# Reordering the two ends of a spectral and windowed-attention kernel: first loads from two queues, zero matmuls ahead of the first product, one pad a step earlier, and output projections in front of a block's last sums

## The chip, the cores and the metric

The kernel runs on one core of a Trainium2 chip. The metric is device time in microseconds for one execution. Five engines matter: TensorE (PE; its weight loads are PEld), VectorE (DVE), ScalarE (ACT), GpSimd (POOL) and SyncE (SP), which issues nearly all of this kernel's DMAs.

## The reference

```python
# x: 2048 x 512; 32 heads of 16; window of 256 keys, causal
g = sigmoid((x * gate_w).sum(-1, keepdims=True))
a = einsum("bsd,ed->bse", x, dft_hid_re);  b = einsum("bsd,ed->bse", x, dft_hid_im)
y = einsum("ts,bse->bte", dft_seq_re, a) - einsum("ts,bse->bte", dft_seq_im, b)
q, k, v = split(x @ wqkv)
scores = where(0 <= i - j < 256, q @ k.T * 16**-0.5, -1e9)
att = (softmax(scores) @ v).reshape(S, D) @ wo
out = g * y + (1 - g) * att
```

So the output is a gated mix of a two-sided Fourier product (real part) and a sliding-window attention with an output projection. Everything is float32. Each large product is made of three matmuls in a faster 32-bit format: both operands are split into a high part (a cast) and a low part (the rest), and the terms high x high, high x low and low x high are summed (`TERMS`).

## The kernel before, in words

**Attention.** Queries are cut into 4 head groups times 32 blocks of 64 positions, 128 blocks in all; the main loop runs over them with index `n`. Per step, four pairs `p` make scores S (`s_pair`, line 319: a query block, padded so that two heads share it, against a ring of keys), and VectorE adds the mask and takes the row maximum, ScalarE the exponential's sum. Eighteen steps behind (`LAG`, `k = n - LAG`) come the transposed scores T (`t_pair`, line 384: a key block in `PAD[1, k]` against the ring of queries), their exponential, and the product with V (`pv`, line 411). `make_pad(i, n)` writes a padded block: for T one half is VectorE's (line 304) and the other is ScalarE's (line 302). In the kernel before, T's first pad is made at the start of step `n = 18` (`k == 0`), each later one a step ahead of its use.

**Dense work.** All else is a generator, `dense()`, that yields between groups of matmuls; `fill(n)` draws a fixed number of them per half pair into the attention loop. It runs the first Q/K product (`qk_first`, line 226), V's blocks (`v_proj`, line 260), the other Q/K products (line 238), the hidden-side Fourier products (line 260 too), and the sequence-side Fourier sums (`c_block`, line 442): 16 output blocks `tb` for the first half, then 16 for the second, each 48 matmuls of 512 columns. What is left of it when the attention loop ends runs by itself.

**The start.** Before that loop, the first pieces of the Q/K weights (`wqk`, four of 128x256) and of x transposed (`xT`, four of 128x512) are loaded in turn from SP's queue, split on ScalarE (line 136 and `split`, line 80) and VectorE (lines 83 and 138), and multiplied.

**The end.** When the attention is done, `attention_done` splits the output projection's weights into `fin`. From then on `add_r` (line 566) combines a block's Fourier sum with the first half's and calls `wo_block`: load the attention output of the block, split it into a buffer named `raw`, 12 matmuls (line 604), mix with line 606, store. One block that had been waiting is projected in front of each.

**What sets the order.** TensorE's order is the order of the trace (`manual_schedule`). On the other engines a planner orders the instructions by its own simulated time, except inside the block at lines 127 to 138. `mark` remembers the last instruction of an engine, and `with behind(...)` or `late(...)` puts what follows behind it in that engine's order. The pool `ev` has 5 buffers, `raw` 2, the split weights `hi` and `lo` 3 each; the PSUM pool `ps_a` has 4 banks shared by S, T and the projections.

Of the kernel before, what the change touches and what calls it, by code (L numbers as in the profile page):

```python
# [14 lines left out]
P = 128  # L15
# [3 lines left out]
NG = 4  # L19
# [4 lines left out]
BIG = 1e30  # L24
SCALE = 0.25
LAG = 18
BEHIND = 4
FILL_FIRST, FILL_PROJ, FILL_SEQ = 3.0, 3.5, 3.6

# [2 lines left out]
def fnet_window_mix(ctx: ExitStack, tc: tile.TileContext, xT, x, wqk, wv, wr, wi, cr, ci, wo, gw, out):  # L32
# [21 lines left out]
    def ld(dst, src):  # L54
        return nc.sync.dma_start(dst, src)

    def store(dst, src):
        mark("sp", ld(dst, src))

    def f(ap):  # L60
        return ap.bitcast(F32)
# [56 lines left out]
    def split_x(ss, dks, act=False):  # L118
        for dk in dks:
            XT[dk, ss] = big.tile([P, 2, 512], F32R, name="big")  # L120
            split(XT[dk, ss][:, 0], XT[dk, ss][:, 1], XRAW.pop((dk, ss)), act)
# [5 lines left out]
    with tc.manual_schedule(engines={mybir.EngineType.Activation, mybir.EngineType.DVE, mybir.EngineType.SP}):  # L127
        wraw, *xraw = [pt_raw() for _ in range(3)]
        wq0 = [st.tile([P, 1024], F32R, name=h) for h in ("hi", "lo")]
        for dk in range(DK):  # L130
            ld(wraw[:, dk * 256:dk * 256 + 256], wqk[0][:, dk * 256:dk * 256 + 256])
            XRAW[dk, 0] = xraw[dk // 2][:, HALVES[dk % 2]]
            ld(XRAW[dk, 0], xT[0, dk])
        for dk in range(DK):
            c = slice(dk * 256, dk * 256 + 256)
            nc.scalar.copy(wq0[0][:, c], wraw[:, c])
            split_x(0, (dk,), True)
            nc.vector.tensor_sub(wq0[1][:, c], wraw[:, c], f(wq0[0][:, c]))


    NPAD = 3
# [51 lines left out]

    def gate_load(j):
        if j == 0:
            ld(gwb, bass.AP(tensor=gw.tensor, offset=gw.offset, ap=[[0, P], [1, D]]))
        GX[j] = st.tile([P, 1024], F32, name="raw", bufs=2)
        for c in range(2):
            ld(GX[j][:, HALVES[c]], x[2 * j + c])
# [275 lines left out]
    def late(fn, *args):  # L475
        with behind("act", "dve"):
            return fn(*args)

    def dense():
        wraw = [load_raw(wv[i]) for i in range(2)]  # L480
        qk_first(wq0)
        wvs = [split_raw(r, True) for r in wraw]
        load_x(1, 0)
        load_x(1, 1)
        yield
        for ss in range(4):
            if ss:
                yield from qk_proj(0, ss, wq0)
            for c in range(4):
                yield from v_proj(ss * 4 + c, wvs)  # L490
                have.add(("v", ss * 4 + c))
                if c == 1:
                    have.add(("qk", 0, ss))
                if ss < 3:
                    if c in (1, 2):
                        late(split_x, ss + 1, (2 * c - 2, 2 * c - 1), ss == 0)
                        if ss < 2:
                            load_x(ss + 2, c - 1)
                elif c == 0:
                    raw = load_raw(wqk[1])  # L500
                    wraw = [load_raw(wi[0])]
                elif c == 2:
                    w = late(split_raw, raw)
        for g in range(1, NG):
            for ss in range(4):
                yield from qk_proj(g, ss, w)
                have.add(("qk", g, ss))
                if g == 1:
                    if ss == 0:
                        wraw.append(load_raw(wi[1]))  # L510
                    elif ss < 3:
                        if ss == 1:
                            ws = []
                        ws.append(late(split_raw, wraw[ss - 1]))
                        if ss == 1:
                            raw = load_raw(wqk[2])
                        else:
                            gate_load(0)
                elif g == 2:
                    if ss == 0:  # L520
                        raw = load_raw(wqk[3])
                        wraw = [load_raw(wr[0])]
                    elif ss == 2:
                        nextw = late(split_raw, raw)
                        wraw.append(load_raw(wr[1]))
                elif ss in (0, 2):
                    if ss == 0:
                        ws = []
                    ws.append(late(split_raw, wraw[ss // 2]))
            if g == 1:  # L530
                for sb in range(16):
                    yield from ab_proj(1, sb, ws)
                    if sb == 1:
                        nextw = late(split_raw, raw)
                    if sb % 2 == 0 and sb < 14:
                        gate_load(sb // 2 + 1)
                    if sb % 2:
                        late(gate, sb - 1)
                        late(gate, sb)
            if g < 3:  # L540
                w = nextw
        ab = {}
        for sb in range(16):
            if sb >= 4:
                ab[sb] = big.tile([P, 2, 512], F32R, name="big")
            yield from ab_proj(0, sb, ws, ab.get(sb))
        for sc in range(4):
            ab[sc] = load_ab(0, sc)
        have.add("proj")
        def store_r(tb, ps):  # L550
            t = ev.tile([P, 512], F32, name="ev")
            nc.scalar.activation(t, ps, AF.Copy, scale=g1[:, tb:tb + 1])
            ld(r_scr[0][tb], t)

        get = c_pieces([*((0, k) for k in (*range(28), 28, 30, 29, 31)),
                        *((1, k) for k in (0, 2, 1, 3, *range(4, 32)))])
        for tb in range(14):
            yield from c_block(get, 0, tb, ab, store_r)
        yield from c_pair(get, 0, 14, ab, store_r, True)
        ab = nxt  # L560
        wait = []

        def add_r(tb, ps):
            r = ev.tile([P, 512], F32, name="ev")
            ld(r, r_scr[0][tb])
            nc.vector.scalar_tensor_tensor(r, ps, g1[:, tb:tb + 1], r, op0=OP.mult, op1=OP.add)
            if FIN:
                if wait:
                    wo_block(wait.pop(0))
                wo_block(tb, r)  # L570
            else:
                ld(r_scr[1][tb], r)
                wait.append(tb)

        yield from c_pair(get, 1, 0, ab, add_r)
        for tb in range(2, 16):
            yield from c_block(get, 1, tb, ab, add_r)
        while wait:
            wo_block(wait.pop(0))

    FIN = []

    def attention_done():
        fin = const.tile([P, 2, 2, 2, 512], F32R, name="fin", tag="ring0")
        for j in range(2):
            raw = st.tile([P, 1024], F32, name="raw", bufs=2)
            ld(raw, wo[j])
            for c in range(2):
                split(fin[:, j, c, 0], fin[:, j, c, 1], raw[:, c * 512:c * 512 + 512])
        FIN.append(fin)  # L590

    def wo_block(tb, r=None):
        if r is None:
            r = ev.tile([P, 512], F32, name="ev")
            ld(r, r_scr[1][tb])
        oraw = ev.tile([P, NG, P], F32, name="ev")
        ld(oraw, o_scr[tb // 4][:, :, tb % 4 * P:tb % 4 * P + P].rearrange("g p t -> p g t"))
        o = st.tile([P, 2, NG, P], F32R, name="raw", bufs=2)
        split(o[:, 0], o[:, 1], oraw[:], True)
        ps = ps_a.tile([P, 512], F32, name="t", tag="st")  # L600
        n = 0
        for g in range(NG):
            for a, b in TERMS:
                nc.tensor.matmul(ps, o[:, a, g], FIN[0][:, g // 2, g % 2, b], start=n == 0, stop=n == 11)  # L604
                n += 1
        nc.vector.scalar_tensor_tensor(r, ps, g0[:, tb:tb + 1], r, op0=OP.mult, op1=OP.add)
        ld(out[tb], r)


    stream = dense()  # L610
# [34 lines left out]
    for n in range(N + LAG + 2):  # L645
# [13 lines left out]
            v_spread(k + 2)  # L659
        if n == 0:  # L660
            make_pad(0, 0)
        if k == 0:
            make_pad(1, 0)
        for p in range(NP):
            if n < N:
                s_pair(n, p)
            fill(n)
            if 0 <= k < N:
                t_pair(k, p)
            if p == 0:  # L670
                make_pad(0, n + 1)
                if k >= 0:
                    make_pad(1, k + 1)
            fill(n)
            if p == 2 and n % 2:
                for j in (k - 2, k - 1):
                    if 0 <= j < N:
                        pv(j)
                if n % 8 == 1 and 1 < n <= N + 1:
                    m_rows(n // 8 - 1)  # L680
                    l_rows(n // 8 - 1)
# [47 lines left out]
```

## Time and profile before

| | |
|---|---|
| median of 3 runs | 880.83 us (879.98 to 882.15) |
| the profiled execution | 881.33 us, span 879.5 us |
| mean granted TensorE clock | 0.996 |
| TensorE busy | 866.5 us, 5184 matmuls |
| VectorE, ScalarE, GpSimd busy | 600.1, 585.3, 385.0 us |
| DMA | 152.13 MB, mean 173 GB/s |

The page gives the busy time of each engine, the span in 40 slices (each digit the busy share of a slice in tenths), and the chain of work that ended last. The list of waits says which engine sat idle, at which line, and who released it: total us, number of times, longest. The timeline has one row per instruction or group: start, duration, engine, line, operation, output and inputs, and in brackets the idle time before it and what ended it. A row of a table by windows has the stretch, its length, the busy time and count of PE, PEld, DVE, ACT and POOL, the granted clock, the DMA engines' share and GB/s. "L260" is line 260 of the kernel.

### The profile page before, as it was taken

To read this page: it belongs to the slowest core of one execution; us is meant where nothing else is said; L and a number is where in the kernel's file an instruction comes from. 1 tells how busy PE (TensorE), PEld (TensorE's weight loads), DVE (VectorE), ACT (ScalarE), POOL (GpSimd) and SP (SyncE) were. 2 spreads that over 40 slices of the span, in tenths; PEclk is the share of its full clock that TensorE was granted. 3 is DMA by queue.
4 is the path that set the end of the run, shared out by engine and by line. 5 is a ranking of instruction groups with operands and counts; after the bars stand their busy time and mean duration, and the time that the engine had idled before them with its cause. 6 is when DMAs were issued, how large, how long until landed. Compare 5 with 4: busy or idle time off the path is not lost.

```text
span 879.5 us, 17216 instructions
## 1 busy us (share of the span) xinstructions
PE 866.5 (99%) x5184; PEld 692.2 (79%) x5184; DVE 600.1 (68%) x1965; ACT 585.3 (67%) x1794; POOL 385.0 (44%) x1069
## 2 busy tenths in 40 slices
PE   7999899999999999999999999999999999999997
PEld 6888678777877878787778787877878777788885
DVE  4688788777887677777777777778776443454342
ACT  5488788889888887888878878888776444100010
POOL 9100165555544447564455566545656664000000
PEclk9999899999999999999999999999999999999999
DMA  7877668775766136543544353579643323455452
GB/s 265 261 228 214 198 205 272 233 237 174 221 207 210 45 99 200 147 138 120 175 131 140 127 148 115 143 230 348 211 143 126 130 92 126 137 174 156 149 159 88
DMA packets 89823, 152.13 MB, mean 173 GB/s; under 512 B 26753, under 2 KB 35457, under 8 KB 89729
## 3 DMA queue, kind: packets, MB, share of 16 engines
q1 hardware_dynamic: 89728, 151.02, 55.0%
q8 instruction: 41, 0.67, 0.3%
q14 instruction: 54, 0.43, 0.2%
HBM read 103.81 MB, written 47.19 MB: 172 GB/s over the span
## 4 chain that ended last, share of the span: by engine, by line
PE 98%; DMA 1%; ACT 1%; issue 0%; DVE 0%; SPq 0%; ACTq 0%
PE dc L442 41%; PE dab L260 10%; PE dqk L238 10%; PE s L319 9%; PE o L411 8%; PE t L384 8%; PE dv L260 5%; PE t L604 5%; PE s L226 1%; DMA ev<-o_scr 1%; PE s L343 0%; PE s L331 0%; DMA pt<-xT 0%; ACT sm L324 0%; ACT raw L80 0%
## 5 line engine op out<-in xcount | busy, mean ns | idle before, releaser
L442 PE MATMUL dc<-big,hi 128*128 128x512 f32 x1024 | 354.9, 395 | 0.0
L390 POOL TENSOR_SCALAR_AFFINE_SELECT pt<-pt 64x128 f32<-64x128 f32 x512 | 192.7, 376 | 292.1 <-ACT pt L385 276.2
L324 ACT ACTIVATE sm<-sm,nm 128x320 f32<-128x320 f32 (+4 forms) x512 | 276.8, 542 | 59.4 <-DVE nm L321 56.7
L321 DVE CUSTOM_DVE_ANT_0 sm<-s,mask 128x320 f32<-128x320 f32 (+4 forms) x512 | 232.3, 462 | 118.3 <-PE s L319 94.0
L385 ACT ACTIVATE pt<-t 128x320 f32<-128x320 f32 (+4 forms) x512 | 208.0, 412 | 81.3 <-PE t L384 78.7
L442 PEld LDWEIGHTS dc<-big,hi 128*128 128x128 f32 x1024 | 186.8, 188 | 28.0 <-issue 1.5
L442 PE MATMUL dc<-big,lo 128*128 128x512 f32 x512 | 202.6, 396 | 0.0
L319 PE MATMUL s<-ring,pad 128*128 128x320 f32 (+4 forms) x512 | 160.7, 314 | 0.0
L394 POOL TENSOR_SCALAR_AFFINE_SELECT pt<-pt 64x128 f32<-64x128 f32 x448 | 160.3, 358 | 0.0
L384 PE MATMUL t<-ring,pad 128*128 128x320 f32 (+4 forms) x512 | 154.8, 302 | 3.0 <-ACT pad L302 2.6
L304 DVE TENSOR_SCALAR pad<-ring,half 96x256 fp32r<-96x256 f32 x384 | 121.8, 359 | 19.7 <-PE t L384 19.2
L319 PEld LDWEIGHTS s<-ring,pad 128*128 128x128 f32 x512 | 96.4, 188 | 38.7 <-issue 9.3
L384 PEld LDWEIGHTS t<-ring,pad 128*128 128x128 f32 x512 | 96.5, 189 | 20.3 <-ACT pad L302 2.9
L442 PEld LDWEIGHTS dc<-big,lo 128*128 128x128 f32 x512 | 96.2, 188 | 16.5 <-issue 1.6
L83 DVE TENSOR_TENSOR lo<-raw,hi 128x512 fp32r<-128x512 f32 x146 | 100.0, 711 | 0.3 <-ACT hi L80 0.3
L324 ACT ACTIVATION_READ_ACCUMULATOR sm<-sm,nm 128x1 f32 x512 | 98.1, 192 | 0.0
L82 DVE CAST hi<-raw 128x512 fp32r<-128x512 f32 x142 | 56.8, 437 | 51.8 <-PE dc L442 31.8
L260 PE MATMUL dab<-hi,big 128*128 128x512 f32 x256 | 91.1, 396 | 0.0
L238 PE MATMUL dqk<-big,hi 128*128 128x512 f32 x240 | 87.3, 399 | 0.0
L80 ACT CAST raw<-ev 128x512 fp32r<-128x512 f32 x16 | 9.9, 622 | 110.0 <-DVE lo L83 72.3
L411 PE MATMUL o<-pt,vpad 128*32 128x320 f32 (+4 forms) x1408 | 78.6, 352 | 0.0
L411 PEld LDWEIGHTS o<-pt,vpad 128*32 128x32 f32 x1408 | 36.0, 109 | 36.9 <-issue 19.8
(79 smaller groups left out, 823.1 us busy)
## 6 DMA issues: line engine op xcount, KB each, us to landing
qk_scr<-hl SPq DMA_DIRECT2D x32, 512.0 KB
ring<-qk_scr SPq DMA_DIRECT2D x32, 512.0 KB
raw<-cr SPq DMA_DIRECT2D x32, 512.0 KB
raw<-ci SPq DMA_DIRECT2D x32, 512.0 KB
ab_scr<-hl SPq DMA_DIRECT2D x20, 512.0 KB
big<-ab_scr SPq DMA_DIRECT2D x20, 512.0 KB
ring<-qk_scr SPq DMA_DIRECT2D x32, 256.0 KB
r_scr<-ev SPq DMA_DIRECT2D x25, 256.0 KB
```

What stands on the lines that cost most here:

```text
L238: nc.tensor.matmul(ps, w[a][:, c:c + 128], XT[dk, ss][:, b], start=n == 0, stop=n == 11)
L260: nc.tensor.matmul(ps, XT[dk, ss][:, a, c * 128:(c + 1) * 128], wh[b], start=n == 0, stop=n == 11)
L304: nc.vector.tensor_scalar(dst, src, half[:96, h:h + 1], None, op0=OP.mult)
L319: nc.tensor.matmul(ps[:, :w], PAD[0, n][:, p], ring[1][:, p, k0:k0 + w], start=True, stop=True)
L321: mark("dve", nc.vector.tensor_tensor_reduce(out=sm[:, :w], in0=ps[:, :w], in1=mask[:, WIN - w:], scale=1.0, scalar=3e38, op0=OP.add, op1= ...
L324: mark("act", nc.scalar.activation(sm[:, :w], sm[:, :w], AF.Exp, bias=nm[:, c], scale=-1.0, accum_out=l[:, c]))
L384: nc.tensor.matmul(ps[:, :w], PAD[1, n][:, p], ring[0][:, p, q0:q0 + w], start=True, stop=True)
L385: nc.scalar.activation(pt[:, p, :w], ps[:, :w], AF.Exp, scale=-1.0)
L390: nc.gpsimd.affine_select(a, a, pattern=[[0, 2], [1, 64]], compare_op=OP.is_ge, fill=0.0, base=0, channel_multiplier=-1)
L394: nc.gpsimd.affine_select(a, a, pattern=[[0, 2], [-1, 64]], compare_op=OP.is_gt, fill=0.0, base=0, channel_multiplier=1)
L411: nc.tensor.matmul(OT[g, sb][32 * p:32 * p + 32, q - sb * 512:e - sb * 512], v2[:, p], pt[:, p, q - q0:e - q0], start=first, stop=kb == 8 ...
L442: nc.tensor.matmul(ps, w[a][:, s8 * 128:(s8 + 1) * 128], ab[SC[i]][:, b], start=i == 0 and a + b == 0, stop=i == 15 and a == 1)
```

## The change

- The first loads: the x blocks 0 and 2 are issued from ScalarE's queue, x 1 and 3 and the weights from SP's. The first x block's high part is cast on VectorE, not on ScalarE.
- A tile of zeros is set by VectorE, and `warm()` issues six matmuls of it ahead of the first product.
- V's weights are loaded behind the last of these loads on SP; their splits are placed behind the first product's evictions (`late`). The gate's weights are loaded behind what SP had been given by then.
- `make_pad(1, 0)` moves from the start of step 18 to the first pair of step 17.
- At the end, `wo_prep` loads and splits the attention output of coming blocks a block ahead, into a tile of 8 slots in the place of the key ring (`ring1`), not in `raw`. `wo_block` runs in front of a block's sums: for the block itself (`half` 0, with the first half's part), and for blocks that were waiting (`half` 1). `add_r` then only adds the sums and stores; for block 15 in two halves, from two queues. Block 10 joins the waiting ones; 11 to 15 have 3, 4, 3, 3 and 3 projections in front.

```diff
+WARM = 6
...
         wq0 = [st.tile([P, 1024], F32R, name=h) for h in ("hi", "lo")]
+        zero = at.tile([P, 512], F32R, name="rl", bufs=1)
+        nc.vector.memset(f(zero[:]), 0.0)
+        for dk in (0, 2, 1, 3):
+            XRAW[dk, 0] = xraw[dk // 2][:, HALVES[dk % 2]]
+            if dk % 2 == 0:
+                nc.scalar.dma_start(XRAW[dk, 0], xT[0, dk])
         for dk in range(DK):
-            ld(wraw[:, dk * 256:dk * 256 + 256], wqk[0][:, dk * 256:dk * 256 + 256])
-            XRAW[dk, 0] = xraw[dk // 2][:, HALVES[dk % 2]]
-            ld(XRAW[dk, 0], xT[0, dk])
+            store(wraw[:, dk * 256:dk * 256 + 256], wqk[0][:, dk * 256:dk * 256 + 256])
+            if dk % 2 == 0:
+                ld(XRAW[dk + 1, 0], xT[0, dk + 1])
         for dk in range(DK):
             c = slice(dk * 256, dk * 256 + 256)
-            nc.scalar.copy(wq0[0][:, c], wraw[:, c])
-            split_x(0, (dk,), True)
-            nc.vector.tensor_sub(wq0[1][:, c], wraw[:, c], f(wq0[0][:, c]))
+            mark("act", nc.scalar.copy(wq0[0][:, c], wraw[:, c]))
+            split_x(0, (dk,), dk > 0)
+            mark("dve", nc.vector.tensor_sub(wq0[1][:, c], wraw[:, c], f(wq0[0][:, c])))
...
         if j == 0:
-            ld(gwb, bass.AP(tensor=gw.tensor, offset=gw.offset, ap=[[0, P], [1, D]]))
+            with behind("sp"):
+                ld(gwb, bass.AP(tensor=gw.tensor, offset=gw.offset, ap=[[0, P], [1, D]]))
...
+    def warm():
+        ps = ps_d.tile([P, 512], F32, name="dv", tag="d")
+        for i in range(WARM):
+            nc.tensor.matmul(ps, zero[:, :128], zero, start=i == 0, stop=i == WARM - 1)
+
     def dense():
-        wraw = [load_raw(wv[i]) for i in range(2)]
+        warm()
+        with behind("sp"):
+            wraw = [load_raw(wv[i]) for i in range(2)]
         qk_first(wq0)
-        wvs = [split_raw(r, True) for r in wraw]
+        wvs = [late(split_raw, r, True) for r in wraw]
...
+        mixed = {}
+
         def add_r(tb, ps):
-            r = ev.tile([P, 512], F32, name="ev")
-            ld(r, r_scr[0][tb])
-            nc.vector.scalar_tensor_tensor(r, ps, g1[:, tb:tb + 1], r, op0=OP.mult, op1=OP.add)
-            if FIN:
-                if wait:
-                    wo_block(wait.pop(0))
-                wo_block(tb, r)
-            else:
+            r = mixed.pop(tb, None)
+            late_r = r is not None
+            if not late_r:
+                r = ev.tile([P, 512], F32, name="ev")
+                ld(r, r_scr[0][tb])
+            for i in range(2 if tb == 15 else 1):
+                c = slice(i * 256, i * 256 + 256) if tb == 15 else slice(0, 512)
+                nc.vector.scalar_tensor_tensor(r[:, c], ps[:, c], g1[:, tb:tb + 1], r[:, c], op0=OP.mult, op1=OP.add)
+                if late_r:
+                    (nc.scalar.dma_start if i else ld)(out[tb][:, c], r[:, c])
+            if not late_r:
                 ld(r_scr[1][tb], r)
                 wait.append(tb)
...
         for tb in range(2, 16):
+            if tb in O:
+                mixed[tb] = wo_block(tb, 0)
+            for w in [w for w in wait if w in O]:
+                wait.remove(w)
+                ld(out[w], wo_block(w, 1))
+            if FIN and tb < 15:
+                for w in (tb + 1, *wait[:-(-len(wait) // (15 - tb))]):
+                    wo_prep(w)
             yield from c_block(get, 1, tb, ab, add_r)
-        while wait:
-            wo_block(wait.pop(0))
...
+        fin = const.tile([P, 4096 + 16], F32R, name="fin", tag="ring0")[:, 16:]
+        fin = fin.rearrange("p (j c h e) -> p j c h e", j=2, c=2, h=2)
+        OS.append(const.tile([P, 8, 2, NG, P], F32R, name="os", tag="ring1"))
...
+    def wo_prep(tb):
         oraw = ev.tile([P, NG, P], F32, name="ev")
         ld(oraw, o_scr[tb // 4][:, :, tb % 4 * P:tb % 4 * P + P].rearrange("g p t -> p g t"))
-        o = st.tile([P, 2, NG, P], F32R, name="raw", bufs=2)
-        split(o[:, 0], o[:, 1], oraw[:], True)
+        O[tb] = OS[0][:, next(slot) % 8]
+        split(O[tb][:, 0], O[tb][:, 1], oraw[:], True)
+
+    def wo_block(tb, half):
+        o = O.pop(tb)
+        r = ev.tile([P, 512], F32, name="ev")
+        ld(r, r_scr[half][tb])
         ps = ps_a.tile([P, 512], F32, name="t", tag="st")
...
-        ld(out[tb], r)
+        return r
...
-        if k == 0:
-            make_pad(1, 0)
...
             if p == 0:
                 make_pad(0, n + 1)
-                if k >= 0:
+                if k >= -1:
                     make_pad(1, k + 1)
```

More of the change, by code (lines that the diff above doesn't have):

```diff
@@ L576, in dense @@
         for tb in range(2, 16):
+            if tb in O:
[6 more added lines that the diff above has]
+                    wo_prep(w)
             yield from c_block(get, 1, tb, ab, add_r)
-        while wait:
-            wo_block(wait.pop(0))
     FIN = []
     def attention_done():
-        fin = const.tile([P, 2, 2, 2, 512], F32R, name="fin", tag="ring0")
+        fin = const.tile([P, 4096 + 16], F32R, name="fin", tag="ring0")[:, 16:]
+        fin = fin.rearrange("p (j c h e) -> p j c h e", j=2, c=2, h=2)
+        OS.append(const.tile([P, 8, 2, NG, P], F32R, name="os", tag="ring1"))
         for j in range(2):
@@ L590, in attention_done @@
         FIN.append(fin)
[L592 to L595, printed above, removed]
+    OS = []
+    O = {}
+    slot = iter(range(99))
+    def wo_prep(tb):
         oraw = ev.tile([P, NG, P], F32, name="ev")
         ld(oraw, o_scr[tb // 4][:, :, tb % 4 * P:tb % 4 * P + P].rearrange("g p t -> p g t"))
-        o = st.tile([P, 2, NG, P], F32R, name="raw", bufs=2)
-        split(o[:, 0], o[:, 1], oraw[:], True)
+        O[tb] = OS[0][:, next(slot) % 8]
[4 more added lines that the diff above has]
+        ld(r, r_scr[half][tb])
         ps = ps_a.tile([P, 512], F32, name="t", tag="st")
```

## The prediction

> **What bounds the kernel now.** I read the page first (busy shares, slices, the chain), then the list of TensorE's waits, then the timeline around each wait.
>
> ```profile
> span 879.5 us, 17216 instructions
> PE 866.5 (99%) x5184; PEld 692.2 (79%) x5184; DVE 600.1 (68%) x1965; ACT 585.3 (67%) x1794; POOL 385.0 (44%) x1069
> PEclk9999899999999999999999999999999999999999
> PE 98%; DMA 1%; ACT 1%; issue 0%; DVE 0%; SPq 0%; ACTq 0%
> ```
> ```profile
> PE s L226 <- ACT big L80: 4.7, 1, 4.7
> PE t L384 <- ACT pad L302: 2.6, 1, 2.6
> PE t L604 <- ACT raw L80: 1.4, 1, 1.4
> ```
>
> TensorE is the chain, and its matmuls are the same before and after but for six of zeros. So there is nothing to win but its idle time and its slow stretches. The second list has all of it: the start (4.7), the first transposed score (2.6), the last projection (1.4), and behind the last matmul a tail. The change touches each.
>
> **The first T (make_pad(1, 0) a step earlier).**
>
> ```profile
> 95.64 0.39 PE L238 MATMUL dqk<-big,hi 128*128 128x512 f32 x1
> 95.87 0.31 PE L319 MATMUL s<-ring,pad 128*128 128x320 f32 x1
> 96.02 0.40 PE L238 MATMUL dqk<-big,hi 128*128 128x512 f32 x1
> 99.02 0.60 PE L384 MATMUL t<-ring,pad 128*128 128x320 f32 x1 [2.60 <-ACT pad L302]
> 99.42 0.63 PE L238 MATMUL dqk<-big,lo 128*128 128x512 f32 x1
> 99.85 0.63 PE L238 MATMUL dqk<-big,hi 128*128 128x512 f32 x1
> ```
> ```profile
> 97.91 0.74 DVE L82 CAST hi<-raw 128x512 fp32r<-128x512 f32 x2
> 98.58 0.34 DVE L304 TENSOR_SCALAR pad<-ring,half 96x256 fp32r<-96x256 f32 x1
> ```
> ```profile
> 99.02:105.02 6.00, 6.00 (x16) 5.04 (x17) 2.17 (x7) 2.39 (x7) 1.09 (x4) 0.50 0.91 235
> ```
>
> The wait is put down to ScalarE's half of the pad, but VectorE's half ends at 98.92, and TensorE starts at 99.02: that is the later one. It stands behind weight splits (97.91). Then comes a second price: from 99.02 to 105.02 the granted clock is 0.50. Those 16 matmuls (ten of 512 columns, six of 320) would take 10 x 0.23 (95.64 to 95.87) + 6 x 0.15 (95.87 to 96.02) = 3.2 us at full clock; they took 6.0, so 2.8 more. The wait costs 2.6 + 2.8 = 5.4 us. In the changed kernel the same two pad pieces are traced behind pair 0 of step 17, so behind what VectorE and ScalarE had been given by then. On VectorE this can be the eviction in the first row below; it ends at 93.47, and T is due at 96.25, so 2.8 us are left for a piece of 0.34.
>
> ```profile
> 92.79 0.68 DVE L90 SCALAR_TENSOR_TENSOR hl<-dqk,hl 128x512 fp32r<-128x512 f32 x1
> ```
>
> Bounds: all of it (-5.4), or nothing if the planner again puts it behind splits (0). I take -5.4, since what it must follow has been done 2.8 us early. Late next are VectorE's reads of the score banks: VectorE is still busy as the gap ends today (97.91 to 98.92), and the four PSUM banks that S and T share cover about two pairs. I take no stall.
>
> The Trainium skill (TensorE: Matmul & The Clock Gate, Why this matters for your kernels) says the clock falls after gaps above about 3 us. Here 2.6 us were followed by 0.50, so the measurement decides; by the rule alone this term would be -2.6 and the sum 877.1.
>
> **The start (two queues, zeros, later V splits).**
>
> ```profile
> 4.10 0.43 SPq L55 DMA_DIRECT2D pt<-xT  x1
> ```
> ```profile
> 1.50:7.50 6.00, 2.78 (x6) 2.00 (x7) 1.26 (x3) 2.90 (x6) 5.68 (x13) 1.00 0.83 250
> ```
> ```profile
> 8.77 0.62 ACT L80 CAST big<-pt 128x512 fp32r<-128x512 f32 x1 [0.22 <-DMA pt<-xT]
> 10.05 2.42 ACT L80 CAST hi<-raw 128x512 fp32r<-128x512 f32 x4 [0.67 <-DMA raw<-wv]
> 12.38 1.09 ACT L86 ACTIVATE hl<-s 128x512 fp32r<-128x512 f32 x2
> 15.60 0.59 ACT L270 COPY ev<-dv 128x512 f32<-128x512 f32 x1 [2.12 <-PE dv L260]
> ```
> ```profile
> 9.42 0.69 DVE L83 TENSOR_TENSOR big<-pt,big 128x512 fp32r<-128x512 f32 x1
> 10.03 0.42 DVE L138 TENSOR_TENSOR lo<-pt,hi 128x256 fp32r<-128x256 f32 x1
> 10.70 2.58 DVE L83 TENSOR_TENSOR lo<-raw,hi 128x512 fp32r<-128x512 f32 x4 [0.26 <-ACT hi L80]
> ...
> 13.80 0.68 DVE L88 TENSOR_TENSOR hl<-s,hl 128x512 fp32r<-128x512 f32 x1
> ```
> ```profile
> 4.72 8.12 PE s L226 x24
> ```
> ```profile
> 12.68 0.39 PE L260 MATMUL dv<-hi,big 128*128 128x512 f32 x1
> ```
>
> Two queues save issue time: the last x block is SP's fifth issue instead of its eighth, so it goes out three issues of 0.43 earlier, near 2.8 instead of 4.10. But the DMA engines are 0.83 busy at 250 GB/s; the eight loads are 4 x (128 + 256) KB = 1.57 MB, 6.3 us from 1.50, so the last cannot land before 7.8; it landed by 8.77. I take 8.3. Behind it stand the cast 0.62, VectorE's 0.69 and 0.42, and four matmuls of 0.23: the first Q/K product ends at 8.3 + 2.6 = 10.9 (bounds 10.4 and 11.4) instead of 12.68, if the array runs at full speed by then. Today the product's 24 matmuls take 8.12 us, 0.34 each against 0.23: part waits, part slow matmuls. For that are the zeros: six at the slow spacing of 0.43 (99.42 to 99.85), 2.6 us from about 1.3, done before 4.72, where the product starts; as long as its first operands are later than 3.9, they cost nothing. If the array stays slow as today, the end stays at 12.68.
>
> What speaks against the gain is `late` on V's weight splits. Today VectorE makes all four low halves (10.70, 2.58) before the Q/K evictions. Now they stand behind both: the second ended at 14.48, 1.80 after the product. The last low half is then ready at 1.80 + 2.58 = 4.38 after the product, and with two matmuls and 0.20 of drain the first V block's copy starts 5.0 after it; today it starts 15.60 - 12.68 = 2.9 after it. So 10.9 + 5.0 = 15.9 against 15.60: +0.3. The bounds are 15.4 (-0.2) and 12.68 + 5.0 = 17.7 (+2.1). I take +0.3, as the middle landing gives it. ScalarE's two issues (0.43 each) stand ahead of its first cast; between 0 and 0.9, I take 0, because the first block's cast moves to VectorE, which idles then, and the first operands are still loading. The gate weights and V's loads, now behind the last wqk load on SP, cost nothing: V's casts come behind the evictions anyway, and the gate is not read until the second group's rows.
>
> The Trainium skill (DMA: Bandwidth & Descriptors, Rules for kernel authors) holds that spreading loads over issuing engines saves only issue time. With the landing left at 8.77 the term would be +0.8 and the sum 874.8.
>
> **The end (projections ahead).**
>
> ```profile
> 851.46 0.62 PE L442 MATMUL dc<-big,hi 128*128 128x512 f32 x2
> ...
> 862.36 8.56 PE L604 MATMUL t<-fin,raw 128*128 128x512 f32 x36
> ...
> 872.29 3.33 PE L604 MATMUL t<-fin,raw 128*128 128x512 f32 x12 [1.37 <-ACT raw L80]
> ```
> ```profile
> 848.85 0.33 SPq L55 DMA_DIRECT2D raw<-ci  x1
> ```
> ```profile
> 855.44 0.69 DVE L83 TENSOR_TENSOR lo<-raw,hi 128x512 fp32r<-128x512 f32 x1
> ...
> 875.66 0.75 DVE L606 SCALAR_TENSOR_TENSOR ev<-t,g,ev 128x512 f32<-128x512 f32 x1 [2.03 <-PE t L604]
> ```
> ```profile
> 876.41:879.50 3.09, 0.00 (x0) 0.00 (x0) 0.00 (x0) 0.00 (x0) 0.00 (x0) 1.00 0.23 85
> ```
>
> All four projections behind the last sums move ahead of them. The last one's wait goes (1.37), and its own stumble: twelve matmuls took 3.33, while 36 took 8.56, so 2.85 for twelve; 0.48 more. That is 1.9 us. The tail of 0.75 + 3.09 stays: two halves of the sum (0.42 each, as VectorE's 256-column row) are no shorter together, and the second half's transfer is at most 0.3 shorter. Bounds: -2.2, and above nothing if the crowd of loads stalls TensorE (rival below). I take -1.9. By the code, tb 10 gets no projection and 11 to 15 get 3, 4, 3, 3, 3 ahead of their sums; each operand is prepared a block (10.9 us) early, for which a load, a cast of 0.62 and a subtraction of 0.69 per projection are enough. The split operands sit in the old key ring, which nothing reads by then. The extra store and reload for tb 10, and up to four loads of o, four of r and four stores a block on SP, are hidden by that block.
>
> **Sum.** The profiled execution took 881.33 (span 879.5, 1.8 around it), 0.5 above the median 880.83 and inside the runs' spread. 881.33 + 0.3 - 5.4 - 1.9 = 874.3.
>
> **Rivals.**
> - *T still waits.* The planner may put the pad behind the splits again, or another wait take its place, with the slow clock after it: 874.3 + 5.4 = 879.7. Against it is the 2.8 us of room. 0.10.
> - *The wait goes, the slow stretch stays,* because the clock falls for another reason: 874.3 + 2.8 = 877.1. But the clock row has one slice under 0.9, the one with this gap, so 0.07. The clock-gate rule above would give this time.
> - *The start's new gap slows the clock.* Between the Q/K product and the first V matmul TensorE idles for two evictions (1.09) and a cast (0.62), and then starves on low halves. If that costs another slow 6 us: 874.3 + 2.8 = 877.1. A 1.37 us wait at the end brought no slow stretch, 2.60 did. 0.10.
> - *The late splits do not bind* (the low halves keep up): 10.9 + 2.9 = 13.8, -1.8 for +0.3: 872.2. 0.10.
> - *Slower: SP's order at the end.* Today a block's second weight piece is issued at 848.85 and split by 856.13; TensorE needs it 24 matmuls after 851.46, at 856.9: 0.8 to spare. If that load queues on SP behind a store that waits for one more projection (2.8), each of blocks 11 to 15 stalls 2.0: 874.3 + 10 = 884.3. It decides for slower from 2.6 late in every block (9.2 in all, to 883.5). Against it: the projections no longer take `raw` buffers from these pieces. 0.07.
>
> **How the numbers follow.** The forecast, 0.56, has its own range 873.0 to 876.0. About 0.3% (2.6 us) is what a measurement of this kernel can tell from no change, so faster means below 878.2. Forecast, starved start, slow stretch and unbound splits are faster, with a little of the first rival: 0.85. Same is the rest of that: 0.08. Slower 0.07. The range is 871.5 to 879.8, from unbound splits to T still waiting.
>
> **What would show it.** T's first matmul follows its neighbour without idle and the clock is 1.00 around 96; Q/K's first product ends near 11 and V's first copy near 16, with VectorE's V splits behind the evictions; 48 projection matmuls stand before the last 48 sums, and no idle between. Wrong would be idle before L384 again, a clock below 1 after the first product, or waits of the last sums for weights.

## The result, and the profile after

The changed kernel takes 879.54 us (median of 21 runs), the kernel before 880.86: ratio 0.9987, 95% interval 0.9981 to 0.9993. That is 1.3 us faster, inside what I had called no change, where 874.3 was forecast; 879.54 still lies under the upper end of the range, 879.8. All three parts of the change moved TensorE's work. Start and end nearly cancel, and most of what the earlier pad won was given back behind it.

First the page of the changed kernel, then the list of TensorE's waits (total us, times, longest):

```profile
span 878.9 us, 17233 instructions
```
```profile
PE t L392 <- ACT pt L393: 2.9, 2, 2.3
PE dv L490 <- DVE rl L132: 1.5, 1, 1.5
PE dv L268 <- ACT hi L81: 1.2, 1, 1.2
PE s L234 <- DVE big L83: 0.6, 1, 0.6
PE dv L268 <- DVE lo L84: 0.3, 1, 0.3
```

The lines moved by some: T is L392 now, V L268, the first product L234, the projections L638, the sums L450. T's wait for its pad and the projections' wait are gone. New are a wait of T for ScalarE's exponential `pt` (2.3), and waits of V's first matmuls for their split weights (1.2 and 0.3).

**The start.** Timeline of TensorE, ScalarE and VectorE, and a table by windows (stretch, length, busy time and count of PE, PEld, DVE, ACT and POOL, granted clock, DMA share, GB/s):

```profile
12.38 0.39 PE L234 MATMUL s<-big,lo 128*128 128x512 f32 x1
13.96 0.49 PE L268 MATMUL dv<-hi,big 128*128 128x512 f32 x1 [1.19 <-ACT hi L81]
...
17.02 1.05 PE L268 MATMUL dv<-hi,big 128*128 128x512 f32 x2
```
```profile
12.12 1.28 ACT L87 ACTIVATE hl<-s 128x512 fp32r<-128x512 f32 x2 [3.50 <-PE s L234]
13.30 2.17 ACT L81 CAST hi<-raw 128x512 fp32r<-128x512 f32 x4
18.96 0.59 ACT L278 COPY ev<-dv 128x512 f32<-128x512 f32 x1 [3.50 <-PE dv L268]
```
```profile
9.48 0.42 DVE L145 TENSOR_TENSOR lo<-pt,hi 128x256 fp32r<-128x256 f32 x1
...
14.04 2.49 DVE L84 TENSOR_TENSOR lo<-raw,hi 128x512 fp32r<-128x512 f32 x4
```
```profile
14.00:17.00 3.00, 2.68 (x8) 1.91 (x9) 2.53 (x5) 1.47 (x3) 3.00 (x3) 0.82 0.90 324
```

All operands of the first product are split by 9.90, yet it ends at 12.6 as before. V's splits then stand behind the evictions, TensorE idles 1.2 us, starves on low halves, and falls to half clock near 16 (two matmuls in 1.05 us, granted clock 0.82 over the stretch). For the first product that column is no help: it reads 1.00 from 5.00 to 9.50, while the matmuls there come 0.43 apart, so the spacing is what tells the speed. V's first copy starts at 18.96, where it was 15.60.

**T, and what came behind it.** Timeline of TensorE, SP's queue and ScalarE, the chain that ended last, and a table by windows:

```profile
99.53 0.31 PE L327 MATMUL s<-ring,pad 128*128 128x320 f32 x1
99.67 0.40 PE L246 MATMUL dqk<-big,hi 128*128 128x512 f32 x1
99.91 0.31 PE L392 MATMUL t<-ring,pad 128*128 128x320 f32 x1
...
117.93 0.41 PE L392 MATMUL t<-ring,pad 128*128 128x320 f32 x1 [2.35 <-ACT pt L393]
```
```profile
102.59 2.69 SPq L56 DMA_DIRECT2D ring<-qk_scr  x4
```
```profile
107.34 9.60 DMA qk_scr<-hl
```
```profile
116.96 0.60 ACT L87 ACTIVATE hl<-dqk 128x512 fp32r<-128x512 f32 x1 [3.61 <-DMA qk_scr<-hl]
```
```profile
105.00:117.00 12.00, 10.59 (x56) 7.83 (x54) 8.94 (x32) 7.94 (x26) 6.82 (x17) 1.00 1.06 282
117.90:122.00 4.10, 4.07 (x16) 2.55 (x20) 2.39 (x8) 4.10 (x14) 2.15 (x8) 0.58 0.88 270
```

T's first matmul follows its neighbour at once (99.91). But a store of an evicted Q/K product (one that was copied out of PSUM), issued at 107.34, lands 9.6 us later, with the DMA engines full (share 1.06). Ahead of it stand four loads of the query and key rings, 1.5 MB, issued from 102.59. `hl`, the tile that is stored, has two buffers, so the next eviction on ScalarE waits 3.6 us for it. Everything behind it on ScalarE waits too, the exponentials of T among it, their PSUM banks stay full, and TensorE idles 2.35 us. A half-clock stretch (0.58) follows.

**The end.** The chain of the changed kernel:

```profile
856.12 8.24 PE t L638 x36
864.37 10.89 PE dc L450 x48
875.28 0.48 DVE ev L588
```

The last projections stand ahead of the last sums, with no idle between.

**The ledger.** TensorE's order is the same in both kernels, so one and the same score matmul can be compared: the one at 95.87 before is at 99.53 after, and so on.

| TensorE against the kernel before, us | just before T (95.87) | at 115.56 | at 131.88 | last matmul's end |
|---|---|---|---|---|
| changed kernel | +3.7 | -1.7 | +2.3 | -0.4 |

So the start costs 3.7, T's pad wins 5.4, the new wait gives back 4.0, the end wins 2.7, and the tail behind the last matmul is 0.2 shorter: -0.6, which is the difference of the two spans (878.9 and 879.5).

### The profile page after: what moved, and what is told of

Same layout as the page of the kernel before. It is cut to its first block, busy times and chain, and to the rows that moved or that the text cites. A ratio compares the mean times of both kernels' runs of the same rounds, so it can differ in the third digit from the quotient of the medians.

```text
span 878.9 us, 17233 instructions
## 1 busy us (share of the span) xinstructions
PE 868.7 (99%) x5190; PEld 694.0 (79%) x5190; DVE 601.4 (68%) x1968; ACT 583.6 (66%) x1793; POOL 386.6 (44%) x1069
## 4 chain that ended last, share of the span: by engine, by line
PE 97%; DMA 1%; DVE 0%; issue 0%; ACT 0%; DVEq 0%; ACTq 0%
PE dc L450 41%; PE dab L268 10%; PE s L327 9%; PE dqk L246 9%; PE o L419 8%; PE t L392 8%; PE dv L268 5%; PE t L638 5%; DMA qk_scr<-hl 1%; PE s L234 1%; PE s L351 0%; DMA pt<-xT 0%; PE s L339 0%; ACT pt L393 0%; DVE lo L84 0%
## 5 line engine op out<-in xcount | busy, mean ns | idle before, releaser
L450 PE MATMUL dc<-big,hi 128*128 128x512 f32 x1024 | 354.8, 395 | 0.0
L450 PEld LDWEIGHTS dc<-big,hi 128*128 128x128 f32 x1024 | 186.9, 188 | 27.8 <-issue 1.5
L450 PE MATMUL dc<-big,lo 128*128 128x512 f32 x512 | 202.6, 396 | 0.0
L392 PE MATMUL t<-ring,pad 128*128 128x320 f32 (+4 forms) x512 | 154.5, 302 | 2.9 <-ACT pt L393 2.9
L392 PEld LDWEIGHTS t<-ring,pad 128*128 128x128 f32 x512 | 96.2, 188 | 20.4 <-ACT pt L393 4.0
L450 PEld LDWEIGHTS dc<-big,lo 128*128 128x128 f32 x512 | 96.2, 188 | 16.4 <-issue 1.6
L268 PE MATMUL dab<-hi,big 128*128 128x512 f32 x256 | 92.1, 400 | 0.0
L81 ACT CAST os<-ev 128x512 fp32r<-128x512 f32 x16 | 9.8, 621 | 84.9 <-DMA ev<-o_scr 80.7
```

What stands on the lines that cost most here:

```text
L268: nc.tensor.matmul(ps, XT[dk, ss][:, a, c * 128:(c + 1) * 128], wh[b], start=n == 0, stop=n == 11)
L392: nc.tensor.matmul(ps[:, :w], PAD[1, n][:, p], ring[0][:, p, q0:q0 + w], start=True, stop=True)
L450: nc.tensor.matmul(ps, w[a][:, s8 * 128:(s8 + 1) * 128], ab[SC[i]][:, b], start=i == 0 and a + b == 0, stop=i == 15 and a == 1)
```

## The experiments

### One part of the change at a time

Three kernels, each the kernel before with one part. The pad alone:

```diff
-        if k == 0:
-            make_pad(1, 0)
...
-                if k >= 0:
+                if k >= -1:
                     make_pad(1, k + 1)
```

> The kernel before with one edit: T's first pad is made a step earlier. Backlog theory: T's first matmul no longer waits (2.6 us of idle and the 2.8 us slow stretch behind it go), but the DMA engines are just as full there as in the changed kernel, so ScalarE's eviction of a Q/K product waits for the landing of an earlier Q/K store, all of ScalarE stands behind it, and TensorE idles about 2.4 us some 16 us later, with a slow stretch behind that: 4.3 of the 5.5 us are given back, about 879.6 against 880.9. Shift theory (the new wait comes from the start being 3.65 us late, which puts the loads of that stretch elsewhere): no new wait, 5.5 us faster, 875.4.

Measured: 880.21, ratio 0.9991 (0.9981 to 1.0). Waits of TensorE, then of ScalarE between 95 and 125:

```profile
PE t L384 <- ACT pt L385: 2.7, 2, 2.4
```
```profile
ACT hl L86 <- DMA qk_scr<-hl: 3.7, 1, 3.7
```

The late start is not needed: the same wait appears with the start untouched. That rules the shift theory out. Only the pad moved, and TensorE is 4.9 us ahead of before at 115.56 and 0.3 ahead at 131.88.

The end alone (`wo_prep`, `wo_block`, `add_r` and `attention_done` as in the change):

> The kernel before with the end part alone. From the traces: the last wait (1.4) and the stumble behind it (0.5) go, the projections' matmuls come at 0.229 instead of 0.233 us (0.8 in 192), and the tail is 0.2 shorter: 2.9 to 3.1 us faster, about 877.9. If a weight piece or SP's order stalls a block's sums, less; the trace of the changed kernel shows no wait there. A part of it could also be owed to the shift by 64 bytes of the projection's weights, which this run contains.

Measured: 878.18, ratio 0.9966 (0.9953 to 0.9979), 2.8 us less. Its trace holds one thing more, at T:

```profile
98.91 0.38 PE L384 MATMUL t<-ring,pad 128*128 128x320 f32 x1 [2.60 <-ACT pad L302]
99.13 0.39 PE L238 MATMUL dqk<-big,lo 128*128 128x512 f32 x1
99.36 0.39 PE L238 MATMUL dqk<-big,hi 128*128 128x512 f32 x1
...
115.90 0.42 PE L384 MATMUL t<-ring,pad 128*128 128x320 f32 x1 [2.67 <-ACT pt L385]
```

T waits 2.60 us for its pad, as in the kernel before, but the matmuls behind it come at full spacing. And the later wait is there, though the pad was not moved: ScalarE waits 3.15 us for the store, TensorE 2.67. The start alone:

> The kernel before with the start part alone (two queues, zeros, V's splits behind the evictions, later gate weights). Late-split theory: the first Q/K product ends no earlier than before (near 12.6), the first V copy starts near 19.0 instead of 15.6, and TensorE is 3.6 us behind from there; T's first wait and its slow stretch are as in the kernel before, so the whole is 3.6 us slower, about 884.5. Rival, that other work hides the late start: within 1 us of before.

Measured: 884.04, ratio 1.0034 (1.002 to 1.0049), 3.1 us more; V's first copy at 18.52. The idle of 1.19 and 0.32 us ahead of V is as in the changed kernel, but no slow stretch follows it here. The parts add up: +3.1, -0.8 and -2.8 make -0.5, beside -1.3 for the whole.

### The start: what stands behind V's late first matmul

The changed kernel with V's splits free:

```diff
-        wvs = [late(split_raw, r, True) for r in wraw]
+        wvs = [split_raw(r, True) for r in wraw]
```

> The changed kernel with one edit: V's weight splits are no longer placed behind the evictions of the first product. Late-split theory: TensorE goes from the first product (end near 12.6) straight into V, no slow stretch near 16 to 19, the first V copy near 15.5 instead of 18.96; 3.6 us less from there on, and 875.9 if nothing is given back later; if the DMA backlog near 115 keeps its absolute time, up to 3.6 of it is given back there. Load theory (it is the two queues that make the start late): the first V copy stays near 18.

Measured: 876.44, ratio to before 0.9946 (0.9931 to 0.996). ScalarE's rows:

```profile
8.96 2.40 ACT L81 CAST hi<-raw 128x512 fp32r<-128x512 f32 x4
12.52 1.28 ACT L87 ACTIVATE hl<-s 128x512 fp32r<-128x512 f32 x2 [1.16 <-PE s L234]
15.92 0.59 ACT L278 COPY ev<-dv 128x512 f32<-128x512 f32 x1 [2.12 <-PE dv L268]
```

The casts fit into the time in which ScalarE waited for the product. V's first copy is back at 15.92, and the whole is 3.1 us under the changed kernel's median (3.6 by the two ratios). One word, `late`, cost about what the whole end part won (2.8).

Next, nine zeros instead of six, with the splits free:

```diff
-WARM = 6
+WARM = 9
```

> The changed kernel with V's splits not placed behind the evictions, and nine matmuls of zeros instead of six, so that they last until the first operands are there (1.53 to about 5.0). Gap theory (the array stays slow until about 9.3 because TensorE idles 0.6 us between the zeros and the product, so that no stretch of about 3.4 us is filled): full spacing 0.23 from about 6, the first product ends near 10.9 instead of 12.6, V's first copy near 14.2, 1.7 us less from there; on the whole 874.7 if the backlog near 115 does not hold it at an absolute time, else within 0.5 of the kernel with six. Zeros theory (matmuls of zeros do not bring the clock up): slow until 9.3 as with six, no change.

Measured: 875.63 (0.994, 0.9923 to 0.9957). TensorE with six zeros (first fence) and with nine (second):

```profile
1.53 2.93 PE L490 MATMUL dv<-rl 128*128 128x512 f32 x6 [1.53 <-DVE rl L132]
...
8.86 0.63 PE L234 MATMUL s<-big,lo 128*128 128x512 f32 x1
...
13.00 0.39 PE L268 MATMUL dv<-hi,big 128*128 128x512 f32 x1
```
```profile
1.53 3.81 PE L490 MATMUL dv<-rl 128*128 128x512 f32 x9 [1.53 <-DVE rl L132]
...
6.78 0.39 PE L234 MATMUL s<-big,lo 128*128 128x512 f32 x1
...
11.80 0.39 PE L268 MATMUL dv<-hi,big 128*128 128x512 f32 x1
```

With the gap closed the array is at full speed from about 6, and V starts at 11.80 instead of 13.00. It holds beyond this pair: in the three traces with nine zeros full spacing begins between 6 and 7.3, in the seven with six zeros whose product starts near 5 it begins between 8.7 and 11.1. So zeros do bring the clock up, if they last until the first operands. By the medians 0.8 of these 1.2 us reach the end, with intervals that overlap; the wait near 115 grows from 2.3 to 2.8.

Without zeros:

```diff
     def dense():
-        warm()
```

> The changed kernel with V's splits not placed behind the evictions and without the matmuls of zeros. Gap theory (six zeros end 0.6 us too early to fill a stretch that brings the clock up): matmuls at 0.43 until about 9.3, V's first matmul near 13.0, both as with six zeros. Rival (six help in part): V's first matmul 0.5 us later or more.

One run, 878.23: V's first matmul at 13.68, matmuls slow until about 11.3, later than the 9.3 expected. By the numbers given this is the rival (0.7 later than with six), but with six zeros that moment varies by 2.4 us from trace to trace (above), and the kernel before, without zeros, has it near 9.5. So whether six help stays open.

The two queues, with nine zeros and free splits:

```diff
-            if dk % 2 == 0:
-                nc.scalar.dma_start(XRAW[dk, 0], xT[0, dk])
...
-            if dk % 2 == 0:
-                ld(XRAW[dk + 1, 0], xT[0, dk + 1])
+            ld(XRAW[dk, 0], xT[0, dk])
```

> Nine matmuls of zeros, V's splits not placed behind the evictions, and the first loads all from SP's queue in the old order. Queue theory (two queues make the first operands late, 4.1 to 4.3 instead of 3.1 for the first weights, as they share the same DMA engines, but the last block earlier): the first product starts 0.3 to 0.5 sooner, its last x block lands near 8.8 instead of 8.0, and as VectorE's low halves behind it end the product, the product ends 0.3 earlier to 0.5 later than with two queues (11.8): the whole within 0.6 of the kernel with two queues (875.6). Rival (two queues are worth what they save in issue time, 1.3 us): 1 us slower.

Measured: 876.59 (0.9952, 0.9935 to 0.9968), 1.0 more than with two queues, with intervals that overlap. The first weights are there at 3.23 instead of 4.04, the last x block is cast at 9.29 instead of 7.97, and V starts at 12.11 instead of 11.80. By this pair two queues are worth 0.3 us at this place (0.16 against the other trace with two queues and nine zeros, where V starts at 11.95); the rest of the 1.0 is not placed. The trace fits the queue theory, the median the rival, and the runs do not decide.

### The wait near 115: what the store waits for

The gate's weights where the planner puts them:

```diff
-            with behind("sp"):
-                ld(gwb, ...)
+            ld(gwb, ...)
```

> The changed kernel with V's splits not placed behind the evictions and the gate's weights loaded where the planner puts them, as in the kernel before (256 KB taken out of the full stretch near 113). Backlog theory: these are 0.7 us of all DMA engines, so ScalarE's wait for the Q/K store shrinks from 3.6 by up to 0.7, and the slow stretch may stay: 0.7 to 3 us faster than the same kernel without this edit (876.4). Rival (the gate's load is behind the store in the queue and takes nothing from it): no change there.

Measured: 880.06 (0.9988, 0.9979 to 0.9998), 3.6 us slower than the kernel without this edit. The planner put this load first of all:

```profile
0.82 0.39 SPq L56 DMA_DIRECT2D gwb<-gw  x1
1.27 0.42 SPq L56 DMA_DIRECT2D pt<-wqk  x1
```
```profile
6.68 0.40 ACT L143 CAST hi<-pt 128x256 fp32r<-128x256 f32 x1 [3.65 <-DMA pt<-wqk]
```

The first weights then land at 6.68 instead of 4.33. That makes the start 3.5 us later. Near 115 ScalarE still waits 3.5 us, so these 256 KB are not the cause there: the rival is right. The miss shows what `behind("sp")` on the gate's load was worth.

The third group's Q/K weights two products later:

```diff
-                        if ss == 1:
-                            raw = load_raw(wqk[2])
-                        else:
-                            gate_load(0)
+                        if ss == 2:
+                            gate_load(0)
+                    else:
+                        raw = load_raw(wqk[2])
```

> The changed kernel with V's splits not placed behind the evictions, and the third group's Q/K weights (512 KB, issued near 102 to 105) loaded two products later. Backlog theory: 512 KB at 200 to 300 GB/s are about 2 us, so the Q/K store that ScalarE waits for lands 2 us sooner; TensorE's wait of 2.3 near 115 goes or falls under 0.5, and with it the slow stretch: 3 to 4.5 us faster than the kernel without this edit (876.4), 872 to 873.4. Rival (the store's long landing is the ring loads' small packets alone): within 0.7 of it.

Measured: 877.65 (0.9967, 0.9955 to 0.9978), 1.2 more, and ScalarE's wait is 4.7. It settles nothing: the planner filled the place with two x loads of 256 KB, issued at 103.66 and 106.25, so as many bytes stood there as before.

The rings' loads. Each ring load of the first head group waits for a step count that protects older ring contents; the first group has none to protect:

```diff
-            if ("qk", g, ss) not in have or n - LAG < 32 * (g - 1) + 8 * ss + 9:
+            if ("qk", g, ss) not in have or g and n - LAG < 32 * (g - 1) + 8 * ss + 9:
```

> The changed kernel with the rings' loads of the first head group freed from the lag rule, so that the last of them (1.5 MB, issued near 102.6 in the changed kernel) goes out some 26 us earlier, behind the Q/K store that it reads. Backlog theory: the Q/K stores issued from 102 on land in about 2 to 4 us instead of up to 9.6, ScalarE's eviction waits for none, TensorE's wait of 2.3 near 115 and the slow stretch behind it go: 4.3 us faster than the changed kernel (879.5), about 875.3, unless the earlier loads hold up something near 76. Rival (the store is slow for another reason than bytes ahead of it): no change.

Measured: 875.18 (0.9934, 0.9919 to 0.9949), 4.4 us faster than the changed kernel. TensorE's waits are those of the start and no others. The window that answers to 105 to 117 above:

```profile
101.00:117.00 16.00, 16.00 (x93) 12.10 (x93) 14.54 (x49) 15.45 (x49) 11.58 (x30) 1.00 0.79 237
```

The DMA share in that stretch is 0.79, ScalarE's evictions wait for no store, TensorE is busy throughout. The backlog was the 1.5 MB of the rings' last loads.

The other side of the same wait is the number of buffers (three for `hl`, three instead of five for `ev` to make room):

> The changed kernel with V's splits not placed behind the evictions, three instead of two buffers for evicted Q/K products, and three instead of five `ev` buffers to make room. Buffer theory: ScalarE's eviction has a free buffer while the second store is still in flight, its wait of 3.6 falls under 1 and TensorE's 2.3 near 115 go; the rows of the end may show new waits for want of `ev` buffers, so only the stretch from 95 to 125 tells. Rival (ScalarE or VectorE is itself behind there): TensorE still waits about 2.3.

One run, 875.5. ScalarE's wait for the store falls from 3.6 to 1.5, not under 1, and TensorE's 2.3 go:

```profile
ACT hl L87 <- DMA qk_scr<-hl: 1.5, 1, 1.5
```

The smaller `ev` pool cost TensorE 0.5 us in a wait of a Q/K matmul for an `ev` copy. So two buffers and a store that lands late make the wait together; either remedy removes TensorE's share.

Did T's wait cover this in the kernel before? The earlier ring loads in the kernel before, alone and with the pad:

> The kernel before with the earlier ring loads alone. Cover theory (in the kernel before, the wait for T's pad and the slow stretch behind it give the DMA engines the time to clear the backlog, so the backlog costs nothing there): within 0.9 us of before. Rival (the backlog costs the kernel before as well): 2 us faster or more.

> The kernel before with T's first pad a step earlier and the earlier ring loads. Cover theory: the pad's gain comes through in full, 5.5 us faster than before, about 875.2, where the pad alone was 0.8 faster; no wait of TensorE between 95 and 125. Rival (something else takes the pad's gain): 879.5 to 880.5, as with the pad alone.

Measured: 879.51 alone (0.9981, 0.9969 to 0.9994) and 875.7 with the pad (0.9949, 0.9932 to 0.9966). The pad is worth 0.8 without the ring loads and 3.8 on top of them, and the wait is gone: TensorE is 6.2 us ahead of before at 131.88 in the profiled execution, of which 0.6 comes from its start. So the ring loads are what takes the pad's gain, as the cover theory says. The earlier loads alone gave 1.5, between its 0.9 and the rival's 2.

What covers them is the slow stretch, as far as the traces go, and not the wait. In the kernel before the ring loads are issued only as the wait ends:

```profile
99.01 2.69 SPq L55 DMA_DIRECT2D ring<-qk_scr  x4
```

| profiled execution | T's wait for its pad, us | lost to the slow clock behind it | TensorE's wait some 17 us later |
|---|---|---|---|
| kernel before | 2.60 | 2.8 | none |
| start alone | 2.60 | about 1.7 (an estimate from granted 0.85 over 99 to 105, 0.86 over 105 to 111) | 1.49 |
| end alone | 2.60 | none (granted 1.00) | 2.67 |

With the same wait, the later one grows as the slow stretch shrinks. These are three single executions, not an experiment, but the times agree. With the earlier ring loads, the three of ten runs at a mean granted clock of 1.0 took 876.8 to 877.7, the seven at 0.996 to 0.998 took 879.2 to 881.0. Of the 13 runs of the kernel before beside them, the four at 1.0 took 879.2 to 881.0 and the others 880.5 to 881.7: there a run without the slow stretch gains little, as it would if the store's wait then takes its place. For runs without a trace that is not shown.

### The rest

The projections' matmuls come at 0.229 us instead of 0.233. Without the shift of their weights by 64 bytes:

```diff
-        fin = const.tile([P, 4096 + 16], F32R, name="fin", tag="ring0")[:, 16:]
+        fin = const.tile([P, 4096], F32R, name="fin", tag="ring0")
```

> The changed kernel with V's splits not placed behind the evictions and without the shift of the projection's weights by 64 bytes. Place theory (the projections' 0.229 instead of 0.233 us comes from that shift): 36 matmuls of a block's projections take 8.4 instead of 8.24, 0.8 in all. Rival (it comes from the attention output lying in the key ring's place, or from its order): still 8.24.

One run, 876.14. Its chain:

```profile
772.54 8.17 PE t L638 x36
780.72 10.92 PE dc L450 x48
```

The place theory is wrong: without the shift the projections are faster still (8.17) and the sums slower (10.92 instead of 10.88), about even over the whole. What made 0.233 into 0.229 was not tried.

All remedies together: free splits, nine zeros, earlier ring loads:

> The same earlier ring loads, with nine matmuls of zeros and V's splits not placed behind the evictions. If the backlog holds TensorE near 115 to 120 whatever comes before, the gains of the start and of T's pad come through in full only here: against the same kernel without the earlier ring loads (875.6) 4 to 4.8 us, about 871.1. Rival (no backlog): 875.6.

Measured: 871.48, ratio 0.9902 (0.9881 to 0.9923), the best here, 9.1 us under the kernel before (880.62 in the same runs). Its profiled execution took 874.98. In that one T waits 2.0 us once, behind an eviction that waits 3.1 us for another store from the same two buffers:

```profile
ACT hl L87 <- DMA ab_scr<-hl: 3.1, 1, 3.1
```

## Why the prediction was wrong

**The first T: right in itself, wrong in what is late next.** The pad's step was right: no wait at T, 5.4 us won by 115.56 (1.7 + 3.7). The step that failed is "Late next are VectorE's reads of the score banks ... I take no stall". Late next was a DMA: the store that frees ScalarE's eviction buffer. I had looked for a successor on the compute engines, though the row I quoted for the slow stretch shows a DMA share of 0.91: the slow stretch behind T was time in which the DMA engines cleared 1.5 MB. As far as three traces show it, the 2.8 us that I counted as T's second price hid a wait of about the same size: in the run of the end alone, which had the gap of 2.60 without the slow stretch, TensorE waited 2.67 for the store instead. With the ring loads moved, the pad's gain stays (875.18 and 875.7 in place of 879.5 and 880.2).

**The start: mis-sized, +0.3 forecast, +3.7 measured.** Two terms failed. First, "the first Q/K product ends at 8.3 + 2.6 = 10.9": the data were there earlier than I took (last split at 9.90, where 8.3 + 1.73 makes 10.0), but the condition behind it, an array at full speed, did not hold. I had written that the zeros end at 3.9 and the first operands come by 4.7, and priced that gap at nothing; nine zeros that close it bring the product's end to 11.8. Second, "the first V block's copy starts 5.0 after it": measured 18.96 - 12.6 = 6.4. The splits behind the evictions gave the order I had worked out, and in the starved stretch the clock fell. That was my rival "the start's new gap slows the clock", at 0.10; its 2.8 us were about 1.4 here. The 5.0 itself was right where the clock held: in the run of the start alone the copy came 18.52 - 13.53 = 5.0 behind the product. So the whole lay above my upper bound, 17.7 for V's first copy, which had allowed for the slow array but not for both. My floor of 7.8 for the last landing was also no floor: it took 250 GB/s for the most that the DMA engines move, and they moved 374 GB/s from 5.00 to 9.50.

**The end: right, a little small.** -1.9 forecast, -2.9 measured with the tail (2.7 + 0.2), -2.8 by itself in a run. The missing 1.0 are 0.8 in the projections' spacing, which I did not foresee, and 0.2 in the tail. The rival with SP's order did not occur: no wait of the sums in the trace.

**The range.** It held the time only by 0.3, and by luck. Its upper end is the first rival, at 0.10, which has the words for what came ("another wait take its place, with the slow clock after it") but no account of which wait. The terms of the profiled execution make 874.3 + 3.4 (start) - 1.0 (end) + 4.0 (the new wait) = 880.7, where it took 880.74; that this is near the rival's 874.3 + 5.4 = 879.7, and that the median lies lower, is no merit of the range. The forecast "faster" at 0.85 was wrong in kind: the whole moved 0.13%.

## What to carry to other kernels

When a wait goes, look for what its time was used for on the DMA queues as well as on the engines: a store that frees a buffer is a dependency of the next writer, and what stands behind that writer on its engine waits too. Here a slow stretch had hidden such a store. An ordering edge ("behind") on work that could have run in another wait is not free; look at what the engine did in that time before. Matmuls of zeros that are to warm the array should last until the first real ones: here nine did, six did not.

## What the runs showed of the hardware that was not expected

The half clock behind a gap is not a fixed price. In the kernel before, 2.60 us of idle at T were followed by 6.0 us at a granted 0.50. In the kernel before with earlier ring loads, the same 2.60 us in the profiled execution were followed by matmuls at 0.23:

```profile
98.51 0.38 PE L384 MATMUL t<-ring,pad 128*128 128x320 f32 x1 [2.60 <-ACT pad L302]
98.72 0.39 PE L238 MATMUL dqk<-big,lo 128*128 128x512 f32 x1
98.96 0.40 PE L238 MATMUL dqk<-big,hi 128*128 128x512 f32 x1
```

The end alone shows the same (above). And the 1.19 and 0.32 us of idle ahead of V were followed by a slow stretch in the changed kernel, but by full spacing in the start alone and in the changed kernel with earlier ring loads. The Trainium skill (TensorE: Matmul & The Clock Gate, Part 1: The HAM clock gate) says that the window in which the array's activity is judged runs freely, so that its phase varies by run. These traces are in keeping with it, but none shows the window itself. My 2.8 us for the slow stretch was one execution's value, and a comparison of single profiles carries about that much.

A load of one 2 KB row spread over 128 partitions, put first in the queue, delayed the first weights behind it from 4.33 to 6.68; only 0.45 of that is their later issue (1.27 instead of 0.82). In the kernel before, the 256 KB of the first x block came 0.96 us after the first weights (3.09 to 4.05).
